# Retention and a mixture of experts in one kernel: slots and gates of quarter rows fetched through DRAM, drains spread over the experts, other capacities

## The chip, the cores and the metric

The kernel runs on one core of one Trainium2 chip. The metric is the device time of one execution in microseconds (us): the median of three timed runs before the change is 395.25 us (395.16 to 395.92). A further run was taken with the hardware profiler, and its own time is given beside its span. Engine names are those of the profile: PE is the matrix engine (PEld its weight loads), DVE the vector engine, ACT the scalar engine, POOL the general one, SP the engine that issues most DMAs; a name with a q (POOLq) is the engine's queue.

## The reference

```
# retention: 8 sequences, 8 heads, 576 positions, 64 wide
scores = q @ k^T / sqrt(64);  ret = scores * gamma_h ** (i - j) for i >= j, else 0
x = (ret @ v) as 4608 rows of 512
# mixture of experts with a skip
active = x @ w_skip > 0;  out = x
e = argmax(x[active] @ w_gate) over 8 experts;  gate = its softmax probability
out[active] = x[active] + gate * (relu(x[active] @ w1[e]) @ w2[e])   # 512 -> 1024 -> 512
```

## The kernel before

**Retention.** The first 158 us compute x, 36 tiles of 128 tokens by 512, and write it to out. On the way each token gets an expert and a rank in it. The experts are then handled in the order of their token counts (the busiest first), each with a fixed number of columns from `CAPS`; tokens beyond a capacity would go to a loop at the end, which runs zero times on the reference's inputs.

**Expert 0** is special: 256 of its rows are gathered and multiplied during the last retention tiles (`up_early`, `down_early`), the rest, `CAPS[0] - 256` rows, is the late block (`up_late`). Its weights come in pieces: ACT makes a high part, and POOL the low part of a half chunk in `lower`, which is called with one or two pieces per retention tile. The two copies of the gathered rows by chunk, xp (L430, POOL), feed the turns `pt_early` (L841) on PE.

**Experts 1 to 7** run through eight chunks f of the hidden layer. A step is an up (12 matmuls into ph) and, one step later, a down (12 matmuls into py): all products are three-term products of high and low parts, so each expert has 192 matmuls that stream its capacity in columns. After an up ACT writes the high part hhi and DVE the low part hlo (L570); the down reads hhi in its first matmul and hlo in its second. Weights of a chunk are loaded by SP (w), split by ACT (whi) and DVE (wlo, L187).

**Quarter rows.** A token's 512 features are handled as four quarters of 128. For an expert e from 2 on, `gather_next` fetches its token rows (xg, POOL indirect DMA), `stow` writes them to DRAM (xr, L1215), `spread` reads them back as quarters (xq, four DMAs on SP's queue, L1225), and `turn_quarters` (DVE, L1239) turns them into the columns of the up. The results of experts 1 to 6 are turned by DVE out of PSUM (yq), scaled by the gates on ACT (`scale_quarters`, L1136), added to xq on DVE (`add_quarters`, L1144), and written by POOL as indirect puts (L1147), 60 in all. `quarter_ids` makes the destination rows qidx and the gates qgate of all experts: 16 matmuls of idf and gate with a selector sel spread them over the partitions (ps_q, L1105), and DVE works on them. `slot_first` broadcasts the first slot's ids by two matmuls (ps_first, L511), for the slots without a token.

**Order.** The order on each engine is written by hand: `at(e, f, place, ...)` hangs an action on step (e, f), place 0 after the up of f, place 1 after the down of f - 1, place 2 after the weights' splits and loads. `keep` holds that order. A group (`new_group`, `in_line`) keeps POOL's indirect DMAs in sequence. A single drain of POOL (L1301) stands at (7, 3, 1).

**End.** After expert 7's last down, py is copied to SBUF (two groups by ACT, two by DVE), turned by 12 transposes into three blocks yn, and DVE makes rs = yn * gate + xg for each (L1188); POOL puts each to out (L1192). All this is `finish`. The loop at L1402 and the end of the kernel (L1498) follow.

Of the kernel before, what the change touches and what calls it, by code (L numbers as in the profile page):

```python
# [11 lines left out]
F32 = mybir.dt.float32  # L12
# [5 lines left out]
ALU = mybir.AluOpType  # L18
# [13 lines left out]
NQD = P // Q  # L32
NBLK = 3

CAPS = (368, 344, 332, 308, 304, 286, 278, 276)
CAP = CAPS[0]
MAXB = -(-NTOK // P)
NW = NE + 1
# [16 lines left out]
LOADED = (6, 8, 10, 11, 12, 13)  # L55
KCUT = 3
LAST = len(GROUPS) - 1
CUT = 2 * P
EARLY = ("sc0", "sc1", "s", "xt0", "xt1", "sc0")
NCUT = 6  # L60
# [5 lines left out]
def kernel(  # L66
# [402 lines left out]

    gidx = const.tile([P, NBLK, NE], I32, tag="gidx", name="gidx")  # L470
    sidx = const.tile([P, NBLK, NE], I32, tag="sidx", name="sidx")
    gate = const.tile([P, NBLK, NE], F32, tag="gate", name="gate")

    def late_ids(ps):

# [21 lines left out]
    def slot_ids(ps):  # L497

        info = ps[:, 0 : NBLK * NE * NCMP].rearrange("s (b e k) -> s b e k", b=NBLK, k=NCMP)
        vec("tensor_copy", raw, info)  # L500
        idf = rt.tile([P, NBLK, NE], F32, tag="idf", name="idf")
# [6 lines left out]
    def slot_first(idf):  # L508

        ps = bank("m", "ps_first")[:, :NE]  # L510
        nc.tensor.matmul(ps, row, idf[0:1, 0, :], start=True, stop=True)  # L511
        return ps

    def slot_rest(idf, first):

        some = rt.tile([P, NBLK, NE], F32, tag="some_slot", name="some_slot")
        head = first.unsqueeze(1).broadcast_to([P, NBLK, NE])
        vec("scalar_tensor_tensor", some, idf, float(P), head, ALU.is_lt, ALU.mult)
        vec("tensor_tensor", some, some, idf, ALU.add)
        vec("tensor_scalar", near, some, float(-P), 0.0, ALU.add, ALU.max)  # L520
        far = rt.tile([P, NBLK, NE], F32, tag="far", name="far")
        vec("tensor_scalar", far, idf, float(P), FAR, ALU.is_lt, ALU.mult)
        vec("scalar_tensor_tensor", sidx, idf, float(-P), far, ALU.add, ALU.add)
        gs = rt.tile([P, NBLK, NE], F32, tag="gs", name="gs")
        vec("tensor_tensor", gs, raw[:, :, :, 2], raw[:, :, :, 3], ALU.add)
        vec("tensor_tensor", gs, gs, raw[:, :, :, 4], ALU.add)
        by = in_order(gs, "gates")
        vec("tensor_reduce", gate, by, axis=AX.X, op=ALU.add)

    row = const.tile([1, P], F32, tag="row", name="row")  # L530
    nc.gpsimd.memset(row, 1.0)
# [65 lines left out]
    with ExitStack() as actx:  # L597
# [322 lines left out]
        for g in range(NT):  # L920
# [18 lines left out]
            if not last:  # L939
                first = decayed(g, pxt)  # L940
                scale(g + 2, first)
                lower(1 if g < NT - 6 else 2, first)
            score(g + (AHEAD_SC if g > 2 else 1))
            if g < 4:
                decays(g + 1)
# [44 lines left out]

    xg0.append(mp.tile([P, DM], F32, tag="xg0_2", name="xg0_2", bufs=1))
    nblock = None
    sel = None
# [3 lines left out]
    qgate = mp.tile([P, NQD * NQE], F32, tag="qgate", name="qgate", bufs=1)  # L997
# [77 lines left out]

    def quarter_tables():

        nonlocal sel
# [21 lines left out]
    def quarter_ids(idf):  # L1100

        ps = bank("m", "ps_q")[:, : 2 * NQD * NQE].rearrange("p (x j i) -> p x j i", x=2, j=NQD)
        for x, t in enumerate((idf, gate)):
            for j in range(NQD):
# [3 lines left out]
        yield  # L1108
        ids = ps[:, 0].rearrange("p j i -> p (j i)")
        t = mp.tile([P, NQD * NQE], F32, tag="t", name="t", bufs=1)  # L1110
        vec("tensor_scalar", t, ids, float(P), 4 * FAR, ALU.is_lt, ALU.mult)
        vec("tensor_tensor", t, t, none, ALU.add)
        vec("scalar_tensor_tensor", t, ids, float(NQD), t, ALU.mult, ALU.add)
        vec("tensor_scalar", qidx, t, quarter, None, ALU.add)
        vec("tensor_copy", qgate, ps[:, 1].rearrange("p j i -> p (j i)"))

    def results(e):
        return mp.tile([P, -(-CAPS[1] // Q), P], F32, tag="yq", name=f"yq_{e}", bufs=1)
# [12 lines left out]

    def scale_quarters(e, yq, gs):

        gates = qgate.rearrange("p (j k e) -> p j k e", j=NQD, e=NE)
# [26 lines left out]
        puts.append(put)  # L1161

    def evacuate(e, py):
        if e == 0:
            return py
        m = CAPS[e]
        yT = results(e).rearrange("p g f -> p (g f)")[:, : NCC * m].rearrange("p (c i) -> p c i", c=NCC)
        for c in range(NCC):
            if c % 2:
                keep(nc.vector.tensor_copy(yT[:, c, :m], py[c][:, :m]))  # L1170
            else:
                keep(nc.scalar.copy(yT[:, c, :m], py[c][:, :m]))
        return yT

    def rows(xg, k, n):
        return xg[k][:n] if isinstance(xg, list) else xg[:n, k, :]

    def finish(e, y, xg, ks, tags=("pt", "m")):
        new_group()
        for k, n in ks:  # L1180
            if e == 0:
                yn = y[k]
            else:
                yn = bank(tags[k % len(tags)], f"yn_{e}_{k}")
                for c in range(NCC):
                    nc.tensor.transpose(chunk(yn[:n], c), y[:, c, k * P : k * P + n], ident)
            rs = mp.tile([P, DM], F32, tag="rs", name=f"rs_{e}_{k}", bufs=3)
            keep(nc.vector.scalar_tensor_tensor(rs[:n], yn[:n], gate[:n, k, e : e + 1], rows(xg, k, n), ALU.mult, ALU.add))  # L1188
            put_rows(e, k, n, rs)

    def put_rows(e, k, n, rs):
# [27 lines left out]
    def spread(e):  # L1219

        n = span(e)
        xq[e] = mp.tile([P, NBLK * NCC, P], F32, tag="xq", name=f"xq_{e}", bufs=2)
        for q in range(NQD):
            rows = xr[e][:, q * P : (q + 1) * P].rearrange("(g a) f -> a g f", a=Q)
            keep(nc.sync.dma_start(xq[e][q * Q : (q + 1) * Q, : n // Q, :], rows))  # L1225

    def copy_rows(e, xg):

        xq[e] = mp.tile([P, NBLK * NCC, P], F32, tag="xq", name=f"xq_{e}", bufs=2)
# [20 lines left out]
    def experts():  # L1250
# [74 lines left out]
        first = []  # L1325
        at(0, NCUT - 2, 1, lambda: first.append(slot_first(idf)))
        at(0, NCUT - 1, 1, lambda: slot_rest(idf, first[0]))
        at(0, NCUT, 1, rank_caps)
        for cur in steps + [None]:
            if cur:  # L1330
# [16 lines left out]
            if last:  # L1347
# [4 lines left out]
                if f == NFC - 1:  # L1352
                    if 0 < e < NE - 1:
                        yq, n = turn_out(e, py[e]), span(e) // Q
                        head, rest = range(NQD), range(NQD, n)
                        at(e + 1, 0, 2, scale_quarters, e, yq, head)
                        at(e + 1, 1, 0, add_quarters, e, yq, xq[e], head)
                        at(e + 1, 1, 0, scale_quarters, e, yq, rest)
                        at(e + 1, 2, 0, add_quarters, e, yq, xq[e], rest)
                    else:  # L1360
                        finish(e, evacuate(e, py[e]), xg[e], blocks(e), ("pt", "m", "ph"))
            for do in between.pop((*place, 1), ()) if place else ():
                do()
            if cur:
# [139 lines left out]
```

## Time and profile before

| | |
|---|---|
| median of 3 runs | 395.25 us (395.16 to 395.92) |
| the profiled execution | 392.77 us, of which its span is 391.1 us |
| mean granted PE clock | 0.995 |
| busy of the span | PE 96%, DVE 68%, POOL 47%, ACT 41% |
| retention; expert 0 and the start of 1 | to about 158 us; to about 186 us |
| experts 1 to 7 | about 186 to 381 us |
| after the last matmul of py | 381 to 391 us |

The shares are means over stages. An engine's idle time counts only where another one waits for it, so the waits of PE and the stretch behind its last matmul are to be read first.

### The profile page before, as it was taken

What the parts mean: (1) busy time and instruction counts of PE and PEld (TensorE: products, weight loads), DVE (VectorE), ACT (ScalarE), POOL (GpSimd) and SP (SyncE); (2) the same over time, 40 slices, a digit from 0 to 9 for tenths busy, and PEclk for the clock granted to TensorE, in tenths of its full rate; (3) what the DMA queues carried; (4) which work ended last, traced back from release to release, by engine and by line L of the source; (5) the groups of instructions that cost most, each with busy time, mean ns of one, the idle gap of its engine ahead of it and who ended that gap; (6) DMA issues with size and microseconds to landing.
All of it is one profiled execution on the core that took longest, in us unless ns stands there. A gap on an engine that the chain in (4) does not pass through costs nothing.

```text
span 391.1 us, 12059 instructions
## 1 busy us (share of the span) xinstructions
PE 374.3 (96%) x4786; PEld 339.8 (87%) x4786; DVE 266.4 (68%) x606; ACT 159.0 (41%) x312; POOL 185.7 (47%) x253
## 2 busy tenths in 40 slices
PE   8989999999899999999999999999999999999991
PEld 4768788788688778888998999999999999999990
DVE  3765694695497945759654876876977788759622
ACT  1213222232223354126242673573564656636520
POOL 5433242342242587259650048547567188470633
PEclk9999999999999999999999999999999999999998
DMA  7999999999999665063999669759678976895001
GB/s 278 389 374 362 359 392 344 341 385 373 386 358 363 215 202 169 26 204 140 290 344 237 173 222 277 244 184 288 227 231 260 279 221 249 251 300 166 30 31 57
DMA packets 50795, 99.97 MB, mean 256 GB/s; under 512 B 6255, under 2 KB 15219, under 8 KB 50736
## 3 DMA queue, kind: packets, MB, share of 16 engines
q1 hardware_dynamic: 41232, 79.58, 62.2%
q0 software_dynamic: 4032, 10.03, 7.9%
q10 hardware_dynamic: 5472, 9.56, 6.5%
q8 instruction: 39, 0.64, 0.7%
q14 instruction: 20, 0.16, 0.1%
HBM read 80.44 MB, written 19.21 MB: 255 GB/s over the span
## 4 chain that ended last, share of the span: by engine, by line
PE 70%; DMA 12%; DVE 6%; POOL 5%; issue 4%; ACT 1%; SPq 1%; POOLq 0%; ACTq 0%; DVEq 0%
PE py L546 19%; PE ph L546 17%; PE pxt L751 8%; PE psc L679 6%; PE px L802 5%; PE ps_s L729 4%; PE pxt L772 4%; DMA out<-yq,qidx 4%; DMA xq<-xr 2%; PE pl L810 2%; DMA xg<-out,near 2%; PE ph_early L546 2%; DMA xg<-out,gidx 2%; DMA xr<-xg 1%; DVE sc L199 1%
## 5 line engine op out<-in xcount | busy, mean ns | idle before, releaser
L1147 POOL DMA_INDIRECT out<-yq,qidx x60 | 69.6, 1160 | 82.6 <-ACT yq L1136 66.8
L187 DVE TENSOR_TENSOR wlo_w<-w,whi_w 128x1024 fp32r<-128x1024 f32 x58 | 70.4, 1214 | 17.6 <-ACT whi_w L184 17.2
L714 POOL TENSOR_TENSOR v<-v,tt_sb 128x512 f32<-128x512 f32 x36 | 37.5, 1042 | 80.5 <-DVE xt L199 58.4
L546 PE MATMUL py<-hlo,whi_w 128*128 128x344 f32 (+6 forms) x224 | 68.1, 304 | 1.4 <-DVE hlo L570 1.4
L546 PE MATMUL ph<-xhi,whi_w 128*128 128x344 f32 (+6 forms) x224 | 67.8, 303 | 0.0
L546 PE MATMUL ph<-xhi,wlo_w 128*128 128x344 f32 (+6 forms) x224 | 67.8, 303 | 0.0
L546 PE MATMUL py<-hhi,whi_w 128*128 128x344 f32 (+6 forms) x224 | 67.8, 303 | 0.0
L546 PE MATMUL py<-hhi,wlo_w 128*128 128x344 f32 (+6 forms) x224 | 67.7, 302 | 0.0
L546 PE MATMUL ph<-xlo,whi_w 128*128 128x344 f32 (+6 forms) x224 | 67.7, 302 | 0.0
L184 ACT CAST whi_w<-w 128x1024 fp32r<-128x1024 f32 x58 | 60.4, 1045 | 4.7 <-DMA w<-w 4.7
L199 DVE TENSOR_TENSOR xt<-pxt,gt_sb 128x256 f32<-128x256 f32 x72 | 27.1, 417 | 36.3 <-PE pxt L772 33.8
L199 DVE TENSOR_TENSOR sc<-psc,mask 128x512 f32<-128x512 f32 x72 | 46.3, 684 | 7.4 <-POOL v L714 4.5
L569 ACT ACTIVATE hhi<-ph 128x344 fp32r<-128x344 f32 (+7 forms) x58 | 24.5, 422 | 60.5 <-PE ph L546 60.5
L804 ACT COPY xn<-px 128x512 f32<-128x512 f32 x36 | 21.1, 587 | 64.4 <-PE px L802 54.2
L546 PEld LDWEIGHTS py<-hlo,whi_w 128*128 128x128 f32 x224 | 42.2, 189 | 2.2 <-DVE hlo L570 2.2
L546 PEld LDWEIGHTS ph<-xhi,whi_w 128*128 128x128 f32 x224 | 42.2, 188 | 0.1
L546 PEld LDWEIGHTS ph<-xlo,whi_w 128*128 128x128 f32 x224 | 42.2, 188 | 0.1
L546 PEld LDWEIGHTS py<-hhi,whi_w 128*128 128x128 f32 x224 | 42.3, 189 | 0.0
L546 PEld LDWEIGHTS py<-hhi,wlo_w 128*128 128x128 f32 x224 | 42.2, 189 | 0.0
L546 PEld LDWEIGHTS ph<-xhi,wlo_w 128*128 128x128 f32 x224 | 42.2, 188 | 0.0
L751 PE MATMUL pxt<-sc,v 128*64 128x128 f32 x576 | 40.0, 275 | 0.3 <-DVE sc L199 0.2
L570 DVE SCALAR_TENSOR_TENSOR hlo<-ph,hhi 128x344 fp32r<-128x344 f32 (+7 forms) x58 | 27.2, 468 | 18.4 <-ACT hhi L569 18.4
(226 smaller groups left out, 621.1 us busy)
## 6 DMA issues: line engine op xcount, KB each, us to landing
w<-w SPq DMA_DIRECT2D x64, 512.0 KB, 4.8
q<-qkv SPq DMA_DIRECT2D x72, 256.0 KB, 5.5
v<-qkv SPq DMA_DIRECT2D x68, 256.0 KB, 5.4
out<-xn ACTq DMA_DIRECT2D x36, 256.0 KB, 5.4
xr<-xg SPq DMA_DIRECT2D x7, 512.0 KB, 4.8
xq<-xr SPq DMA_DIRECT2D x12, 144.0 KB, 5.1
xq<-xr SPq DMA_DIRECT2D x8, 176.0 KB, 6.8
xq<-xr SPq DMA_DIRECT2D x8, 160.0 KB, 5.8
```

The source lines that it names most:

```text
L184: cast = nc.scalar.copy(hi, t)
L187: ins = nc.vector.tensor_tensor(lo, t, hi.bitcast(F32), ALU.subtract)
L199: ins = getattr(nc.vector, name)(*args, **kw)
L546: nc.tensor.matmul(ps, x, y, start=first and n == 0, stop=last and n == 3 * len(terms) - 1)
L569: keep(nc.scalar.activation(hi, ph, AF.Relu))
L570: keep(nc.vector.scalar_tensor_tensor(lo, ph, 0.0, hi.bitcast(F32), ALU.max, ALU.subtract))
L679: nc.tensor.matmul(psc[r][halves[c], a, k0:], q[halves[r], 1, a, k0 : k0 + D], q[halves[r], 0, a, k0:], start=a == 0, stop=a == NPR - 1, s ...
L714: ins = nc.gpsimd.tensor_tensor(v, v, vt_sb[:, place(g), :].unsqueeze(2).broadcast_to([P, H, D]), ALU.mult)
L751: nc.tensor.matmul(pxt[a % 2][halves[j], a // 2, :], v[:, head(a, r), :], sc[:, r, a, :], start=a < 2, stop=t == 0 and a >= NPR - 2, skip_ ...
L802: nc.tensor.transpose(px[:, c * P : (c + 1) * P], xt_t[b][:, c, o * P : (o + 1) * P], ident)
L804: nc.scalar.copy(xn, px)
L1147: nc.gpsimd.indirect_dma_start(out=rows, out_offset=bass.IndirectOffsetOnAxis(ap=ids[:, g % NQD, g // NQD, e : e + 1], axis=0), in_=yq[:, ...
```

## The change

It does five things. (1) `slot_first` and the matmuls ps_q go. The slots' ids and gates lie in one tile, `slots`, which SP writes to DRAM after stow(1) at (0, 7, 1) and reads back in four DMAs at (1, 1, 0), so that each partition has the ids and gates of its four quarters; `quarter_ids` works on these at (1, 3, 0). The id of a slot without a token is taken from the partition's own first slot. (2) Drains of POOL stand at (e, 5, 1) for e = 2 to 6 beside the one at (7, 3, 1). (3) Expert 7 ends in `finish_last`: three column groups are turned and added first and the fourth after them, ACT copies the fourth group in two pieces, and DVE copies one group only. (4) `CAPS` changes. (5) The last retention tiles call `lower` no more before the copies of xp, so those pieces go behind them. Besides, `add_quarters` for the rest of the quarters moves from (e + 1, 2, 0) to (e + 1, 1, 2).

```diff
-CAPS = (368, 344, 332, 308, 304, 286, 278, 276)
+CAPS = (380, 344, 320, 310, 300, 288, 278, 268)
...
-    gate = const.tile([P, NBLK, NE], F32, tag="gate", name="gate")
+    slots = const.tile([P, 2, NBLK, NE], F32, tag="slots", name="slots")
+    gate = slots[:, 1]
...
-        head = first.unsqueeze(1).broadcast_to([P, NBLK, NE])
+        head = idf[:, 0:1, :].broadcast_to([P, NBLK, NE])
...
-                lower(1 if g < NT - 6 else 2, first)
+                if g < NT - 3:
+                    lower(1 if g < NT - 6 else 2, first)
...
-        sel = mp.tile([P, DM], F32, tag="rs", name="sel", bufs=3).rearrange("p (j i) -> p j i", j=NQD)
-        for j in range(NQD):
-            part = ident[:, j * Q : (j + 1) * Q].unsqueeze(1).broadcast_to([P, NQD, Q])
-            pool("tensor_copy", sel[:, j].rearrange("p (q a) -> p q a", a=Q), part)
...
-                nc.tensor.matmul(
-                    ps[:, x, j, :], sel[:, j, :], t.rearrange("p k e -> p (k e)"), start=not (x or j), stop=True, skip_group_check=True
-                )
...
+    def store_slots():
+        kept = dp.tile([P, 2 * NQE], F32, tag="slots", name="kept", bufs=1)
+        keep(nc.sync.dma_start(kept, slots.rearrange("p x k e -> p (x k e)")))
+        return kept
+    def quarter_slots(kept):
+        rows = kept.rearrange("(j a) i -> a j i", a=Q)
+        for q in range(NQD):
+            keep(nc.sync.dma_start(qslot[q * Q : (q + 1) * Q], rows))
...
+    def finish_last(e, y, xg, ks):
+        yn = [bank(tag, f"yn_{e}_{tag}") for tag in ("pt", "m", "ph")]
+        rs = [mp.tile([P, DM], F32, tag="rs", name=f"rs_{e}_{k}", bufs=3) for k, n in ks]
+        cuts = (0, NCC - 1), (NCC - 1, NCC)
+        for c0, c1 in cuts:
+            for k, n in ks:
+                for c in range(c0, c1):
+                    nc.tensor.transpose(chunk(yn[k][:n], c), y[:, c, k * P : k * P + n], ident)
+        new_group()
+        for k, n in ks:
+            for c0, c1 in cuts:
+                out, a, b = (
+                    t.rearrange("p (q c b) -> p q c b", q=NQD, c=NCC)[:, :, c0:c1] for t in (rs[k][:n], yn[k][:n], xg[:n, k, :])
+                )
+                keep(nc.vector.scalar_tensor_tensor(out, a, gate[:n, k, e : e + 1], b, ALU.mult, ALU.add))
+            put_rows(e, k, n, rs[k])
...
-        at(NE - 1, 3, 1, new_group)
-        at(NE - 1, 3, 1, lambda: tc.keep_in_program_order(nc.gpsimd.drain()))
+        for e in range(2, NE):
+            at(e, 3 if e == NE - 1 else 5, 1, new_group)
+            at(e, 3 if e == NE - 1 else 5, 1, lambda: tc.keep_in_program_order(nc.gpsimd.drain()))
...
-        ids = quarter_ids(idf)
-        at(1, 0, 0, next, ids)
-        at(1, 1, 0, next, ids, None)
+        kept = []
+        at(0, NFC - 1, 1, lambda: kept.append(store_slots()))
+        at(1, 1, 0, lambda: quarter_slots(kept[0]))
+        at(1, 3, 0, quarter_ids)
...
-                        at(e + 1, 2, 0, add_quarters, e, yq, xq[e], rest)
+                        at(e + 1, 1, 2, add_quarters, e, yq, xq[e], rest)
```

## Rows read from the trace of the kernel before

**Rows 1.** Page, part 4: the chain of waits by engine, shares of the span.
```profile
PE 70%; DMA 12%; DVE 6%; POOL 5%; issue 4%; ACT 1%; SPq 1%; POOLq 0%; ACTq 0%; DVEq 0%
```
**Rows 2.** Stretch of experts 1 to 7: length, busy by engine, clock, DMA share, GB/s.
```profile
218.00:380.80 162.80, 162.14 (x1178) 161.57 (x1177) 120.50 (x229) 88.46 (x178) 88.57 (x88) 1.00 0.69 215
```
**Rows 3.** Chain in time (start, us, what): blocks at 344 and 278 columns.
```profile
222.31 1.90 PE py L546 x12
...
351.24 1.55 PE ph L546 x12
```
**Rows 4.** Timeline of POOL (start, us, operation): low parts and copies of xp.
```profile
142.05 1.40 POOL L862 TENSOR_TENSOR wlo_w<-w,whi_w 128x256 fp32r<-128x256 f32 x2
143.40 1.16 POOL L430 COPY xp<-xg 128x512 f32<-128x512 f32 x2
```
**Rows 5.** Timeline of PE at the same place (brackets: idle before, and releaser).
```profile
144.06 0.33 PE L841 MATMUL pt_early<-ident,xp 128*128 128x128 f32 x1 [0.51 <-POOL xp L430]
144.61 0.33 PE L841 MATMUL pt_early<-ident,xp 128*128 128x128 f32 x1 [0.23 <-POOL xp L430]
```
**Rows 6.** Timeline of PE: ps_first.
```profile
176.51 0.38 PE L511 MATMUL ps_first<-idf,row 1*128 1x8 f32 x2
```
**Rows 7.** Stretch of ps_q, line 1105 alone: length, PE and PEld busy, clock, DMA.
```profile
188.47:190.17 1.70, 1.70 (x16) 1.70 (x16) 1.00 1.04 399
```
**Rows 8.** Chain in time: POOL's copies for the selector.
```profile
175.92 0.97 POOL sel L205 x4
```
**Rows 9.** Page, part 5: casts of weights (busy, mean ns, idle before, releaser).
```profile
L184 ACT CAST whi_w<-w 128x1024 fp32r<-128x1024 f32 x58 | 60.4, 1045 | 4.7 <-DMA w<-w 4.7
```
**Rows 10.** Timeline of DVE: the first turn of expert 2.
```profile
213.19 0.55 DVE L1239 STREAM_TRANSPOSE xt<-xq 128x352 f32<-128x352 f32 x1 [1.81 <-DMA xq<-xr]
```
**Rows 11.** Timeline of PE: the down that follows.
```profile
214.19 0.42 PE L546 MATMUL py<-hlo,whi_w 128*128 128x344 f32 x1 [0.73 <-DVE hlo L570]
```
**Rows 12.** Waits of PE (us in total, times, longest).
```profile
PE py L546 <- DVE hlo L570: 1.4, 3, 0.7
```
**Rows 13.** Stretch before that turn, columns as in rows 2.
```profile
186.00:216.00 30.00, 29.27 (x185) 28.39 (x184) 16.47 (x26) 9.87 (x16) 11.42 (x12) 1.00 1.07 295
```
**Rows 14.** Page, part 3: SP's DMA queue (packets, MB, share of 16 engines).
```profile
q1 hardware_dynamic: 41232, 79.58, 62.2%
```
**Rows 15.** Timeline of DVE: hlo and rest add in experts 2 and 7.
```profile
231.83 0.50 DVE L570 SCALAR_TENSOR_TENSOR hlo<-ph,hhi 128x332 fp32r<-128x332 f32 x1
232.24 1.08 DVE L1144 TENSOR_TENSOR yq<-yq,xq 128x896 f32<-128x896 f32 x1
...
365.05 0.44 DVE L570 SCALAR_TENSOR_TENSOR hlo<-ph,hhi 128x276 fp32r<-128x276 f32 x1
365.41 0.81 DVE L1144 TENSOR_TENSOR yq<-yq,xq 128x640 f32<-128x640 f32 x1
366.14 1.22 DVE L187 TENSOR_TENSOR wlo_w<-w,whi_w 128x1024 fp32r<-128x1024 f32 x1
```
**Rows 16.** Timeline of PE: the matmuls that read these hlo first.
```profile
233.34 0.31 PE L546 MATMUL py<-hlo,whi_w 128*128 128x332 f32 x1
...
365.69 0.29 PE L546 MATMUL py<-hlo,whi_w 128*128 128x276 f32 x1
```
**Rows 17.** Line 1301: duration ns min/median/max, first and last start.
```profile
L1301 POOLq DRAIN  x1: 13579/13579/13579, 369.9 to 369.9; - x1
```
**Rows 18.** Timeline of POOL behind the drain.
```profile
383.50 0.10 POOL L205 MEMSET step_on<- 128x1 f32 x1 [7.28 <-issue]
384.33 0.98 POOL L1192 DMA_INDIRECT out<-rs,sidx  x1 [0.73 <-DVEq L1402]
```
**Rows 19.** Line 1498, columns as in rows 17: drains at the kernel's end.
```profile
L1498 POOLq DRAIN  x3: 46/103/297, 389.9 to 390.8; - x3
```
**Rows 20.** Timeline of POOL: the shortest idle between a gather and the next puts.
```profile
338.10 1.01 POOL L1147 DMA_INDIRECT out<-yq,qidx  x1 [4.62 <-ACT yq L1136]
```
**Rows 21.** Timeline of DVE: the three rs of expert 7.
```profile
381.93 2.06 DVE L1188 SCALAR_TENSOR_TENSOR rs<-yn,gate,xg 128x512 f32<-128x512 f32 x3 [0.42 <-PE yn L1186]
```

More of the change, by code (lines that the diff above doesn't have):

```diff
@@ L57 @@
 LAST = len(GROUPS) - 1
+XQ = 2
 CUT = 2 * P
@@ L500, in slot_ids @@
         vec("tensor_copy", raw, info)
-        idf = rt.tile([P, NBLK, NE], F32, tag="idf", name="idf")
+        idf = slots[:, 0]
         vec("scalar_tensor_tensor", idf, raw[:, :, :, 0], float(P), raw[:, :, :, 1], ALU.mult, ALU.add)
@@ L506, in slot_ids, with slot_rest @@
         return idf
[L508 to L514, printed above, removed]
+    def slot_rest(idf):
         some = rt.tile([P, NBLK, NE], F32, tag="some_slot", name="some_slot")
-        head = first.unsqueeze(1).broadcast_to([P, NBLK, NE])
+        head = idf[:, 0:1, :].broadcast_to([P, NBLK, NE])
         vec("scalar_tensor_tensor", some, idf, float(P), head, ALU.is_lt, ALU.mult)
@@ L528, in slot_rest @@
         vec("tensor_reduce", gate, by, axis=AX.X, op=ALU.add)
-    row = const.tile([1, P], F32, tag="row", name="row")
-    nc.gpsimd.memset(row, 1.0)
     near = const.tile([P, NBLK, NE], I32, tag="near", name="near")
@@ L992 @@
     nblock = None
-    sel = None
     NQE = NBLK * NE
@@ L996 @@
     qidx = mp.tile([P, NQD * NQE], I32, tag="qidx", name="qidx", bufs=1)
-    qgate = mp.tile([P, NQD * NQE], F32, tag="qgate", name="qgate", bufs=1)
+    qslot = mp.tile([P, NQD, 2 * NQE], F32, tag="qslot", name="qslot", bufs=1)
     quarter = mp.tile([P, 1], F32, tag="quarter", name="quarter", bufs=1)
@@ L1076, in quarter_tables @@
     def quarter_tables():
-        nonlocal sel
-        sel = mp.tile([P, DM], F32, tag="rs", name="sel", bufs=3).rearrange("p (j i) -> p j i", j=NQD)
-        for j in range(NQD):
-            part = ident[:, j * Q : (j + 1) * Q].unsqueeze(1).broadcast_to([P, NQD, Q])
-            pool("tensor_copy", sel[:, j].rearrange("p (q a) -> p q a", a=Q), part)
         p = pidx[:, 0:1]
@@ L1098, in quarter_tables, with quarter_ids @@
             pool("tensor_scalar", beyond[:, :, :, e], slot, float(CAPS[e]), 4 * FAR, ALU.is_ge, ALU.mult)
[L1100 to L1104, printed above, removed]
-                nc.tensor.matmul(
-                    ps[:, x, j, :], sel[:, j, :], t.rearrange("p k e -> p (k e)"), start=not (x or j), stop=True, skip_group_check=True
-                )
-        yield
-        ids = ps[:, 0].rearrange("p j i -> p (j i)")
-        t = mp.tile([P, NQD * NQE], F32, tag="t", name="t", bufs=1)
+    def store_slots():
[6 more added lines that the diff above has]
+            keep(nc.sync.dma_start(qslot[q * Q : (q + 1) * Q], rows))
+    def quarter_ids():
+        ids = qslot[:, :, :NQE]
+        t = mp.tile([P, NQD, NQE], F32, tag="t", name="t", bufs=1)
         vec("tensor_scalar", t, ids, float(P), 4 * FAR, ALU.is_lt, ALU.mult)
-        vec("tensor_tensor", t, t, none, ALU.add)
+        vec("tensor_tensor", t, t, none.rearrange("p (j i) -> p j i", j=NQD), ALU.add)
         vec("scalar_tensor_tensor", t, ids, float(NQD), t, ALU.mult, ALU.add)
-        vec("tensor_scalar", qidx, t, quarter, None, ALU.add)
-        vec("tensor_copy", qgate, ps[:, 1].rearrange("p j i -> p (j i)"))
+        vec("tensor_scalar", qidx.rearrange("p (j i) -> p j i", j=NQD), t, quarter, None, ALU.add)
     def results(e):
@@ L1132, in scale_quarters @@
     def scale_quarters(e, yq, gs):
-        gates = qgate.rearrange("p (j k e) -> p j k e", j=NQD, e=NE)
+        gates = qslot[:, :, NQE:].rearrange("p j (k e) -> p j k e", e=NE)
         for g in gs:
@@ L1163, in evacuate @@
     def evacuate(e, py):
-        if e == 0:
-            return py
         m = CAPS[e]
@@ L1168, in evacuate, with finish @@
         for c in range(NCC):
-            if c % 2:
+            if c == 1:
                 keep(nc.vector.tensor_copy(yT[:, c, :m], py[c][:, :m]))
             else:
-                keep(nc.scalar.copy(yT[:, c, :m], py[c][:, :m]))
-        return yT
-    def rows(xg, k, n):
-        return xg[k][:n] if isinstance(xg, list) else xg[:n, k, :]
-    def finish(e, y, xg, ks, tags=("pt", "m")):
+                for c0, c1 in ((0, P), (P, m)) if c == NCC - 1 else ((0, m),):
+                    keep(nc.scalar.copy(yT[:, c, c0:c1], py[c][:, c0:c1]))
+        return yT
+    def finish_last(e, y, xg, ks):
[6 more added lines that the diff above has]
+                    nc.tensor.transpose(chunk(yn[k][:n], c), y[:, c, k * P : k * P + n], ident)
         new_group()
         for k, n in ks:
[L1181 to L1186, printed above, removed]
+            for c0, c1 in cuts:
[4 more added lines that the diff above has]
+            put_rows(e, k, n, rs[k])
+    def finish(e, yn, xg, ks):
+        new_group()
+        for k, n in ks:
             rs = mp.tile([P, DM], F32, tag="rs", name=f"rs_{e}_{k}", bufs=3)
-            keep(nc.vector.scalar_tensor_tensor(rs[:n], yn[:n], gate[:n, k, e : e + 1], rows(xg, k, n), ALU.mult, ALU.add))
+            keep(nc.vector.scalar_tensor_tensor(rs[:n], yn[k][:n], gate[:n, k, e : e + 1], xg[k][:n], ALU.mult, ALU.add))
             put_rows(e, k, n, rs)
@@ L1221, in spread @@
         n = span(e)
-        xq[e] = mp.tile([P, NBLK * NCC, P], F32, tag="xq", name=f"xq_{e}", bufs=2)
+        xq[e] = mp.tile([P, NBLK * NCC, P], F32, tag="xq", name=f"xq_{e}", bufs=XQ)
         for q in range(NQD):
@@ L1227, in copy_rows @@
     def copy_rows(e, xg):
-        xq[e] = mp.tile([P, NBLK * NCC, P], F32, tag="xq", name=f"xq_{e}", bufs=2)
+        xq[e] = mp.tile([P, NBLK * NCC, P], F32, tag="xq", name=f"xq_{e}", bufs=XQ)
         for k, n in blocks(e):
@@ L1319, in experts @@
         at(1, 0, 0, spread, 1)
-        ids = quarter_ids(idf)
-        at(1, 0, 0, next, ids)
-        at(1, 1, 0, next, ids, None)
+        kept = []
+        at(0, NFC - 1, 1, lambda: kept.append(store_slots()))
+        at(1, 1, 0, lambda: quarter_slots(kept[0]))
+        at(1, 3, 0, quarter_ids)
         at(0, 0, 0, down_early, NCUT - 1)
         at(0, 1, 1, split_raw, 1)
-        first = []
-        at(0, NCUT - 2, 1, lambda: first.append(slot_first(idf)))
-        at(0, NCUT - 1, 1, lambda: slot_rest(idf, first[0]))
+        at(0, NCUT - 1, 1, slot_rest, idf)
         at(0, NCUT, 1, rank_caps)
@@ L1358, in experts @@
                         at(e + 1, 1, 0, scale_quarters, e, yq, rest)
-                        at(e + 1, 2, 0, add_quarters, e, yq, xq[e], rest)
+                        at(e + 1, 1, 2, add_quarters, e, yq, xq[e], rest)
+                    elif e:
+                        finish_last(e, evacuate(e, py[e]), xg[e], blocks(e))
                     else:
-                        finish(e, evacuate(e, py[e]), xg[e], blocks(e), ("pt", "m", "ph"))
+                        finish(e, py[e], xg[e], blocks(e))
             for do in between.pop((*place, 1), ()) if place else ():
```

## The prediction

> **What bounds the kernel now.** I read the chain of waits first, then the stretches of time, then the timelines of the places that the diff touches. The chain is mostly TensorE [rows 1]. In the expert stage PE is busy 162.14 of 162.80 us [rows 2]: what counts there is a matmul taken away, or a wait put in front of one. Blocks of 12 matmuls follow each other with no gap, and their length goes with the columns: 1.90 us at 344, 1.55 at 278 [rows 3], so 0.35 / 66 = 0.0053 us per column and block, and 16 blocks per expert make 0.085 us per column of a capacity. After the last matmul the end is POOL's: a drain, then three puts one behind the other (rows below). So every edit is priced either on PE's path or in this tail. All prices come from the profiled execution (392.77 us, a span of 391.1 and 1.7 around it); the median of the timed runs is 2.5 above it, and I subtract the sum from the median.
>
> **The change, part by part.**
>
> *Low parts behind the copies of xp.* Two POOL low parts run from 142.05 to 143.45, ahead of the two copies of xp [rows 4], and PE waits 0.51 and 0.23 for these copies, with only a few matmuls between the waits [rows 5]. Behind the copies, the low parts no longer delay them: at most 1.4. The gathered rows that the copies read must have landed as well, which these rows don't show, so I take -1.1, between the waits (-0.7) and the low parts (-1.4). The low parts moved are read by the up products of expert 0 several us later; that lead, by the code, is their cover. If it were gone, the 1.4 would come back.
>
> *Capacities.* Experts 1 to 7 lose 12 + 4 + 8 and gain 2 + 2 columns: 20 net, 20 x 0.085 = -1.7. The late block of expert 0 grows from 112 to 124 rows: 24 matmuls with 24 columns more, 24 with 12 more, and two whole ups with 12 more; at 0.0053 / 12 us per column and matmul that is 0.25 + 0.13 + 0.13 = +0.5. Expert 2's span falls from 352 to 320 rows, so one put goes.
>
> *ps_first.* Two short matmuls, 0.38 together, of which PE loses 0.3: -0.3 [rows 6]. The DVE operations behind it stay.
>
> *Quarters' slots and gates.* The 16 matmuls ps_q fill PE from 188.47 to 190.17 [rows 7]: -1.7. POOL also loses the four copies that built their selector, 0.97 [rows 8], and so it gathers expert 2's rows sooner. DVE loses one small copy. SP gains five issues, some 0.5 each, ahead of spread(2) and of weights. The weights are loaded well ahead: of 58 casts two waited for one, 4.7 in all [rows 9]; that lead covers the issues, and without it their 2 us would stand before PE. The new cost is in the DMA. Expert 2's turned rows (xq) are already late: DVE idles 1.81 for them, the low part hlo stands behind that turn on DVE [rows 10], and PE waits 0.73 for hlo [rows 11]. The three waits of PE on hlo sum to 1.4 [rows 12]; one follows at the next turn, one is at xq of expert 7. The stretch before it has the DMA engines at a share of 1.07 [rows 13]: this xq lands when the transfers ahead of it have passed, not when PE asks. PE arrives there 1.1 + 0.3 + 1.7 - 0.5 = 2.6 earlier. The xq comes earlier by its sooner gather (the 1.1 and about 1 for the selector) and by its smaller capacity, 2.2 in all, less what the new small transfers take. These are 128 pieces of 192 bytes into DRAM and 4 x 128 back. By bytes (123 KB at the 295 GB/s of that stretch [rows 13]) they take 0.4; at the mean packet time of the main queue (62.2% of 16 x 391.1 us over 41,232 packets: 94 ns [rows 14]) 640 / 16 x 94 ns = 3.8, though its packets are some ten times as large. No row shows a packet of this size, so I take 1.0, nearer the end by bytes, and keep both. The wait then grows by 2.6 - 2.2 + 1.0 = +1.4 (0.8 to 4.2).
>
> The Trainium skill (DMA: Bandwidth & Descriptors, Specifications) says that below 512 bytes a DMA does a read-modify-write and misses line rate. That speaks for the dear end; no row of this kernel separates it, and by it alone this term would be the +4.2.
>
> *Rest of the quarters added one step sooner.* Before, DVE ran low part of the weights, hlo, rest add. Now the add stands ahead of hlo. There is no gap to hold it: hlo follows its predecessor at once in expert 7 (no idle is noted), ends at 365.49, and the add hands over 0.73 after its start [rows 15]. PE needs this hlo in the second matmul of its down, at 365.69 [rows 16]: 0.20 of slack, so a wait of 0.53. In expert 2 hlo ends at 232.33, the add takes 1.08 in full and somewhat less to the next start, and PE reads at 233.34: 0 [rows 15, 16]. The six experts by the same sum: 0, 0.56, 0.30, 0.71, 0.55, 0.53, together +2.65 (0 to +3.2; 0 if ACT's work shifts so that a gap opens). These waits stand in front of PE one expert at a time, and nothing gives them back but xq of expert 7, which then comes in time: -0.5, about a third of [rows 12]. The puts start only about 0.4 sooner, off the path.
>
> *Drains.* One drain at 369.9 lasts 13.58 us in the queue [rows 17]. Its part behind POOL's last put is the idle 7.28 that ends at 383.50, followed by 0.73 before the first put [rows 18]. At the end three more indirect DMAs are drained, and the longest of three drains takes 0.297 against 0.046 for the shortest [rows 19]: 0.084 per DMA. Before the first drain 87 indirect DMAs were issued: 87 x 0.084 = 7.3, the idle. So I read it as a cost per DMA since the last drain. The six drains then have 29, 13, 13, 13, 9 and 9 DMAs behind them: 2.4, 1.1, 1.1, 1.1, 0.8, 0.8. The first five fall in POOL's idle between a gather and the next expert's puts, whose shortest is 4.62 [rows 20]; queued behind them are only these puts. The last ends long before PE does.
>
> *Last turns by column group.* Without the drain, the first put waits for its rs only. Before, the three rs run from 381.93 for 2.06 [rows 21], so the first is ready at 382.68 and a put could start near 382.8, 1.5 before 384.33 [rows 18]. The two cuts let the first part of rs start before the fourth column group is copied, perhaps 0.2 sooner; they also make PE turn that group last, and if a reader of part of the bank waits for all of it, 0.3 is lost. The puts keep their spacing. I take -1.5 (-1.2 to -1.8).
>
> **The sum.** -1.1 - 1.7 + 0.5 - 0.3 - 1.7 + 1.4 + 2.65 - 0.5 - 1.5 = -2.25. Forecast: 395.25 - 2.25 = 393.0.
>
> **The rivals.**
>
> *A, the drain has a fixed price.* If one drain costs 7.3 whatever stands before it, the last one again ends after PE: issued at about 375 it is done near 382.5, and the tail gains about 0.6 in place of 1.5. The drains in the shorter gaps delay puts by up to 2.7, and the next expert's results need the buffer that these empty, which I put at +0.8. Sum -0.6: 394.7. For it: only one long drain was ever seen. Against it: the short drains, which fit the count. The Trainium skill (GPSIMD Engine Reference, 2.1 Instruction dispatch) gives the first call of newly loaded code about 6 us with no instruction shown; by it the drain's price would be paid once, earlier, and the sum would stand as forecast.
>
> *B, the rest add is hidden.* If DVE finds a gap, the +2.65 goes: -4.9, 390.35. Against it: no idle in the rows at hlo. For it: PE's blocks shift against ACT's scaling in every expert.
>
> *C, slower: the small transfers hold back xq of expert 2.* Place: the first turn of expert 2, in the stretch where the engines are full. At 94 ns per piece the wait grows by 4.2 in place of 1.4: -2.25 + 2.8 = +0.55, and with the rest adds at their upper bound (+3.2) +1.1: 396.3. It decides from some 80 ns per piece on, where the gains are used up. For it: the saturation; against it: the pieces are a tenth of the mean packet.
>
> *D, the change loses its cover in the tail:* the last drain or the evacuation by ACT alone of the fourth group delays rs, and the tail gains nothing: -0.75, 394.5, within the noise.
>
> **How the numbers follow.** Forecast 0.50 (its own range 391.8 to 394.3), B 0.17, A 0.10, D 0.08, C 0.15. A difference of 0.2%, 0.8 us, is about what a measurement of this kernel tells from none. A and D count mostly as no change, C as slower in 0.11 and no change in 0.04; a twentieth of the forecast's share falls under 0.8. Faster 0.70, same 0.18, slower 0.12. The range reaches from somewhat below B, 390.0, to just short of C, 395.9.
>
> **What would show it.** Right: no ps_first and ps_q on PE; the copies of xp start near 142.1; PE's waits on hlo grow from 1.4 to about 5 in all, some six of them at the third step of an expert, with the rest add ahead of hlo on DVE; six drains of 2.4, about 1 and under 1 us; the first last put within 0.2 of the first rs. Wrong: drains of 7 us each (A), no wait at the third step (B), xq of expert 2 landing at its old time or later (C), a first put long after its rs (D). A PE that waits somewhere else for weights, after SP's five issues, would break the sum in a way that I have priced at nothing.

## The result, and the profile after

The changed kernel is slower: 1.0105 of the time before (95% interval 1.0068 to 1.0142), 4.2 us at a median of 396.5 for the kernel before in the same comparison. 393.0 was forecast, and a range that ended at 395.9. The profiled execution has a span of 398.3 us and a mean granted clock of 0.991. Ratios compare fast runs, those within 1.5% of the fastest of their kernel; three of the profiles below (112 late rows, last put of 16 rows, one drain) are of slower runs, and of these only single waits and stretches are read.

The two spans differ by 7.2 us, more than the medians do. The table cuts them by the starts of PE's first matmuls of each stretch (by the puts at the end), after less before:

| stretch | before | after | |
|---|---|---|---|
| retention, up to the px ahead of the early turns | 142.89 | 145.53 | +2.64 |
| to the first early turn (pt_early) | 1.17 | 0.49 | -0.68 |
| to the first late up of expert 0 | 23.53 | 26.63 | +3.10 |
| to the first up of expert 1 | 19.01 | 18.73 | -0.28 |
| to the first up of expert 2 | 33.72 | 35.80 | +2.08 |
| experts 2 to 7 | 160.54 | 160.66 | +0.12 |
| first turn of the last rows to the first put | 3.47 | 2.55 | -0.92 |
| last put to the end | 4.17 | 5.33 | +1.16 |

The first row is not the change's: in the 14 profiles of this study that stretch took 141.6 to 148.3, with nearly the same code in it, and the profile of before is among the short ones. The rest sums to +4.6, near the +4.2 of the timed runs. That nearness is in part luck: each kernel has one profile, and other rows vary too (experts 2 to 7 took 160.7 to 162.7 in the six profiles with the rest add and the capacities of the changed kernel there). Two stretches hold most of the loss, and in neither had the forecast put a price of that size; the end adds 1.2.

Page of after, part 4, the chain by engine, against [rows 1]: PE's share fell from 70% to 52%, and DMA's rose from 12% to 22%. By the same page 9 of these 22 points are q<-qkv, a load of the retention, which the change doesn't touch.
```profile
PE 52%; DMA 22%; DVE 9%; issue 5%; ACT 5%; POOL 3%; SPq 2%; POOLq 1%; ACTq 0%; DVEq 0%
```
Waits of PE in after (us in total, times, longest), against [rows 12]. The second line was not there before.
```profile
PE py L540 <- DVE hlo L564: 4.3, 5, 2.5
PE pt L1055 <- ACT xp L431: 2.7, 1, 2.7
...
PE py L540 <- ACT hhi L563: 0.9, 1, 0.9
```
**The late rows of expert 0.** Timeline of POOL in before and in after: the gather of the late rows takes 2.47 us to issue in place of 1.08.
```profile
160.65 1.08 POOL L435 DMA_INDIRECT xg<-out,gl  x1 [3.30 <-DVE gl L199]
```
```profile
162.74 2.47 POOL L436 DMA_INDIRECT xg<-out,gl  x1 [3.32 <-DVE gl L200]
```
DMA issues of before and of after (last number: us from issue to landing):
```profile
xg<-out,gl POOLq DMA_INDIRECT x1, 3.4
```
```profile
xg<-out,gl POOLq DMA_INDIRECT x1, 7.2
```
Timeline of PE there: the turn of these rows waits 2.67 for their copy, which follows the landing.
```profile
170.64 0.54 PE L1055 MATMUL pt<-ident,xp 124*128 124x124 f32 x3 [2.67 <-ACT xp L431]
```
**Expert 1.** Timeline of DVE in after, against [rows 10]: it stands 7.49 us in front of quarter_ids, for the slots read back from DRAM. The weights' low part and hlo are queued behind. The wait for xq of expert 2 that follows is only 0.92. The four reads take SP 3.46 us to issue (timeline of SP) and land a median of 9.4 us behind their issue.
```profile
213.49 0.21 DVE L200 TENSOR_SCALAR t<-qslot 128x96 f32<-128x96 f32 x1 [7.49 <-DMA qslot<-kept]
...
218.28 0.51 DVE L1240 STREAM_TRANSPOSE xt<-xq 128x320 f32<-128x320 f32 x1 [0.92 <-DMA xq<-xr]
```
```profile
202.21 3.46 SPq L1099 DMA_DIRECT2D qslot<-kept  x4
```
```profile
qslot<-kept SPq DMA_DIRECT2D x4, 24.0 KB, 9.4
```
Timeline of PE there, against [rows 11]:
```profile
213.34 0.43 PE L540 MATMUL py<-hhi,whi_w 128*128 128x344 f32 x1 [0.86 <-ACT hhi L563]
216.28 0.42 PE L540 MATMUL py<-hlo,whi_w 128*128 128x344 f32 x1 [2.51 <-DVE hlo L564]
```
Two stretches of it (length, busy by engine, clock, DMA share, GB/s): PE is busy 0.90 of 4 us, and in the next four the granted clock is 0.58, a mean of its two levels, 2.4 and 1.2 GHz. The wait costs a second time there. At the wait for the late rows the clock of this profile stays at 1.00.
```profile
212.00:216.00 4.00, 0.90 (x5) 0.38 (x3) 2.34 (x6) 2.69 (x4) 0.00 (x0) 1.00 0.85 205
216.00:220.00 4.00, 3.73 (x14) 3.73 (x15) 2.95 (x6) 0.46 (x1) 0.00 (x0) 0.58 1.01 367
```
**The other parts.** Early turns (timeline of PE, against [rows 5]): no wait for xp is left.
```profile
146.03 1.04 PE L835 MATMUL pt_early<-ident,xp 128*128 128x128 f32 x8
```
Rest add (timeline of DVE in expert 7, against [rows 15]): add first, then hlo, which PE gets 0.67 late.
```profile
371.81 0.82 DVE L1137 TENSOR_TENSOR yq<-yq,xq 128x640 f32<-128x640 f32 x1
372.55 0.43 DVE L564 SCALAR_TENSOR_TENSOR hlo<-ph,hhi 128x268 fp32r<-128x268 f32 x1
```
```profile
373.03 0.39 PE L540 MATMUL py<-hlo,whi_w 128*128 128x268 f32 x1 [0.67 <-DVE hlo L564]
```
The tail (timeline of POOL, against [rows 18]): behind the last drain POOL is idle 1.51 in place of 7.28 and then waits for rs, not for the drain. The first rs starts at 389.24 (timeline of DVE), just behind the turn of the fourth column group of its block (388.93 to 389.20), though its own three groups were turned by 388.4.
```profile
384.48 0.10 POOL L206 MEMSET step_on<- 128x1 f32 x1 [1.51 <-issue]
390.40 0.98 POOL L1193 DMA_INDIRECT out<-rs,sidx  x1 [5.82 <-DVE rs L1182]
```
Behind the five drains in the experts POOL is idle 4.98, 4.19, 3.12, 5.04 and 3.12; two of them:
```profile
263.43 0.10 POOL L206 MEMSET step_on<- 128x1 f32 x1 [4.98 <-issue]
...
344.56 0.10 POOL L206 MEMSET step_on<- 128x1 f32 x1 [5.04 <-issue]
```
The first rs:
```profile
389.24 0.88 DVE L1182 SCALAR_TENSOR_TENSOR rs<-yn_pt,slots,xg 128x384 f32<-128x384 f32 x2 [1.50 <-PE yn_pt L1175]
```

### The profile page after: what moved, and what is told of

Read it like the earlier page. It is cut to its first block, busy times and chain, and to the rows that moved or that the text cites. A ratio compares the mean times of both kernels' runs of the same rounds, so it can differ in the third digit from the quotient of the medians.

```text
span 398.3 us, 12026 instructions
## 1 busy us (share of the span) xinstructions
PE 372.9 (94%) x4768; PEld 337.7 (85%) x4768; DVE 266.2 (67%) x599; ACT 159.0 (40%) x313; POOL 183.8 (46%) x252
## 4 chain that ended last, share of the span: by engine, by line
PE 52%; DMA 22%; DVE 9%; issue 5%; ACT 5%; POOL 3%; SPq 2%; POOLq 1%; ACTq 0%; DVEq 0%
PE py L540 15%; PE ph L540 14%; DMA q<-qkv 9%; PE pxt L745 5%; DMA out<-yq,qidx 4%; PE psc L673 3%; PE ps_s L723 3%; PE pxt L766 3%; PE px L796 3%; ACT yq L1129 3%; DVE yq L1120 2%; DMA qslot<-kept 2%; DMA xg<-out,near 2%; DMA xg<-out,gl 2%; PE pl L804 1%
## 5 line engine op out<-in xcount | busy, mean ns | idle before, releaser
L564 DVE SCALAR_TENSOR_TENSOR hlo<-ph,hhi 128x344 fp32r<-128x344 f32 (+7 forms) x58 | 27.3, 471 | 25.0 <-ACT hhi L563 24.7
```

Source lines behind the costliest of these rows:

```text
L564: keep(nc.vector.scalar_tensor_tensor(lo, ph, 0.0, hi.bitcast(F32), ALU.max, ALU.subtract))
```

## The experiments

Theory 1, formed on the trace: DVE's wait for the slots is the loss. Rivals: the xq of expert 2 is late whoever waits; the rest adds are the loss; the late block of 124 rows is. All ratios are to the kernel before, and each kernel has one profile.

**Ids later.**
```diff
-        at(1, 3, 0, quarter_ids)
+        at(1, 7, 0, quarter_ids)
```


> quarter_ids moved from (1, 3, 0) to (1, 7, 0), all else as changed. Theory 1 (DVE stands in quarter_ids waiting for qslot, idle 7.5 us, and the low parts behind it hold PE up for 5.4 us): the idle before quarter_ids on DVE goes, PE waits on hlo of expert 1 no longer than the wait for xq of expert 2 lasts, some 2 to 3 us, and the time is about 2.5 us below that of the changed kernel, ratio to before near 1.004. Rival 2 (the small transfers hold back xq of expert 2, whoever waits for them): xq of expert 2 still lands about 5 us after PE needs it, no gain. Rival 3 (the rest adds ahead of hlo are the loss): nothing changes, ratio 1.010.


1.0112 (1.0073 to 1.0151): no gain. DVE's wait for the slots is gone, but xq of expert 2 is turned 26.9 us after expert 1's first up, as in after, and DVE waits for it:
```profile
219.70 0.51 DVE L1240 STREAM_TRANSPOSE xt<-xq 128x320 f32<-128x320 f32 x1 [1.75 <-DMA xq<-xr]
```
PE's waits in expert 1 fall only from 3.4 us (2.5 for hlo, 0.9 for hhi) to 2.6, and the stretch from 35.8 to 35.0. Theory 1 falls as the whole cause: behind the wait for the slots stood one for xq.

**Slots behind spread(2).**
```diff
-        at(1, 1, 0, lambda: quarter_slots(kept[0]))
-        at(1, 3, 0, quarter_ids)
+        at(1, 3, 0, lambda: quarter_slots(kept[0]))
+        at(2, 0, 0, quarter_ids)
```


> quarter_slots behind spread(2), at (1, 3, 0), and quarter_ids at (2, 0, 0). Theory 1: no wait for qslot on DVE at all and xq of expert 2 comes some 2 us sooner than with the ids alone moved, since SP issues its four reads before the small ones; PE waits in expert 1 for about 1 us or less; 4.5 us below the changed kernel, ratio to before about 0.998. Rival 2: the same gain, but with the ids alone moved there was none. Rival 3: ratio stays 1.010.


1.0190 (1.0137 to 1.0243), a miss: not faster. The stretch from expert 1 to 2 is 34.3 in place of 35.8, but the first turn of xq comes at 27.3, and the turn of the late rows still waits 2.6. By time it is 3.4 us slower than the changed kernel, which its profile doesn't explain.

**Rest add back.**
```diff
-                        at(e + 1, 1, 2, add_quarters, e, yq, xq[e], rest)
+                        at(e + 1, 2, 0, add_quarters, e, yq, xq[e], rest)
```


> The rest add of the quarters back at (e + 1, 2, 0), behind hlo, all else as changed. Rival 3: PE's waits at the third step of experts 2, 4, 5 and 7 (0.5, 0.6, 0.9, 0.95) go, 2.9 us below the changed kernel, ratio about 1.003, while the wait for qslot stays. If theory 1 were all of the loss: no change, ratio 1.010. Both causes can hold side by side.


1.0052 (1.0008 to 1.0096). Expert by expert, 2 to 7, the stretches are shorter than in after by 0.44, 0, 0.57, 0.89, 0 and 0.73: 2.6 us. The timed gain is 2.1, but the intervals of the two ratios overlap, so only the stretches show it. Of PE's five waits on hlo two are left, both in expert 1.
```profile
PE py L540 <- DVE hlo L564: 3.4, 2, 3.0
```

**Both.** The two edits above together.


> Slots behind spread(2), ids at (2, 0, 0) and the rest add back at (e + 1, 2, 0). If both causes hold and add up: 7 us below the changed kernel, 3 us below the kernel before, ratio about 0.992. If the rest add matters little: as with the slots alone, about 0.998. If neither is the cause: 1.010.


1.0072 (1.0038 to 1.0107): not additive, and not below 1. In this profile the turn of the late rows waits 2.8, xq of expert 2 is turned 28.1 after the first up, and the stretch is 36.25. Something else was still in all four kernels.

**Late block of 112 rows.**
```diff
-CAPS = (380, 344, 320, 310, 300, 288, 278, 268)
+CAPS = (368, 344, 320, 310, 300, 288, 278, 268)
```


> The changed kernel with the first capacity back at 368, so that the late block has 112 rows in place of 124; the rest as changed. Theory 4 (a gather of 124 rows, no multiple of 16, is the loss before expert 1: its issue takes 2.5 us in place of 1.1, it lands 7.2 us after it in place of 3.4, and PE waits 2.7 for the late turn): the issue takes 1.1 again, the wait of the late turn goes, the stretch from the early turns to the late up is 23.5 us in place of 26.6 to 29.3; at least 3 us below the changed kernel, ratio about 1.002. Rival 5 (the low parts moved behind the copies hold POOL or PE up there): the stretch stays near 27, and the time falls by the 0.4 of the columns only.


1.0050 (1.0009 to 1.0091), 2.2 us below the changed kernel where 3 were expected, and the intervals overlap. The wait of the late turn is gone, the issue of the gather is 1.08 and the stretch to the late up 24.6.

**Last put of 16 rows.**
```diff
-CAPS = (380, 344, 320, 310, 300, 288, 278, 268)
+CAPS = (380, 344, 320, 310, 300, 288, 278, 272)
```


> The changed kernel with the last capacity 272 in place of 268: the last put has 16 rows in place of 12. In all five profiles with 268 the end came 5.0 to 5.6 us after the start of the last put, against 4.2 with 20 rows before. Theory 6 (the number of rows of that put makes its landing longer): back to about 4.2, less 0.3 for four more columns, 0.8 us below the changed kernel, ratio about 1.008. Rival 7 (it is the code after it, or chance): 5.3 stays, ratio 1.011.


1.0137 (1.0079 to 1.0195); the end comes 5.2 after the last put, so the number of its rows is not what made it longer.

**One drain.**
```diff
-        for e in range(2, NE):
-            at(e, 3 if e == NE - 1 else 5, 1, new_group)
-            at(e, 3 if e == NE - 1 else 5, 1, lambda: tc.keep_in_program_order(nc.gpsimd.drain()))
+        at(NE - 1, 3, 1, new_group)
+        at(NE - 1, 3, 1, lambda: tc.keep_in_program_order(nc.gpsimd.drain()))
```


> The changed kernel with the single drain at (7, 3, 1), the five others taken out. Theory 8 (a drain costs about 0.08 us for each indirect DMA since the last one): POOL is idle for some 7 us behind its last put before the three last ones, the first of which starts 3.4 us after the first turn in place of 2.55, or 1 us later; ratio about 1.013. Rival 9 (the drains between delay the puts and the gathers, and cost time): faster than the changed kernel, by up to 2 us.


1.0209 (1.0144 to 1.0273). Timeline of POOL: the idle of 7.20 is back, for 86 DMAs 0.084 each. It delays the first put by 0.6 (3.15 after the first turn in place of 2.55); the rest of its time is hidden by PE's last down and the turns. By time this kernel is 4.1 us slower than the changed one, and the intervals just miss each other: the trace accounts for 0.6 of it, and the rest is open.
```profile
397.54 0.10 POOL L206 MEMSET step_on<- 128x1 f32 x1 [7.20 <-issue]
398.37 0.98 POOL L1193 DMA_INDIRECT out<-rs,sidx  x1 [0.73 <-DVE rs L1182]
```

**Five parts on the kernel before.** No slots through DRAM, no earlier rest add, 112 late rows.
```diff
-CAPS = (368, 344, 332, 308, 304, 286, 278, 276)
+CAPS = (368, 344, 320, 310, 300, 288, 278, 272)
...
-        head = first.unsqueeze(1).broadcast_to([P, NBLK, NE])
+        head = idf[:, 0:1, :].broadcast_to([P, NBLK, NE])
...
-                lower(1 if g < NT - 6 else 2, first)
+                if g < NT - 3:
+                    lower(1 if g < NT - 6 else 2, first)
...
+                    elif e:
+                        finish_last(e, evacuate(e, py[e]), xg[e], blocks(e))
```
The six drains are those of the changed kernel.


> The kernel before with five parts of the change: low parts behind the copies of xp, no ps_first, six drains, the last turns by column group, and the capacities 368, 344, 320, 310, 300, 288, 278, 272; without the slots through DRAM, the larger late block and the earlier rest add. If theories 1 (or its rival 2), 3 and 4 name all that was lost: 0.7 + 0.3 + 0.9 + 1.4 below the kernel before, some 3 us, ratio about 0.992. If one of the parts kept is a loss: 1.0 or more.


0.9953 (0.9906 to 0.9999): faster than the changed kernel, and than the kernel before by 1.9 us, just clear of none, where some 3 were expected. Some of the missing 1.1 can be seen: the early turns start 0.68 sooner, but the stretch from them to the late up is 24.16 in place of 23.53. PE comes sooner to a matmul that needs a mask of the routing (mks) from DVE and waits longer there (waits of PE before, then here):
```profile
PE ps_m L281 <- DVE mks L199: 0.4, 1, 0.4
```
```profile
PE ps_m L281 <- DVE mks L199: 1.1, 1, 1.1
```

**Late block of 108 rows.**
```diff
-CAPS = (380, 344, 320, 310, 300, 288, 278, 268)
+CAPS = (364, 344, 320, 310, 300, 288, 278, 268)
```


> The changed kernel with the first capacity at 364: a late block of 108 rows, fewer than the 112 of before, but no multiple of 16. Theory 4a (it is the multiple of 16): the gather of the late rows issues for about 2.5 us and lands some 7 us after its start as with 124 rows, PE waits about 2.7 us for the late turn. Rival 4b (it is the larger number of rows): 1.1 us, no wait, as with 112.


1.0100 (1.0057 to 1.0143). Between the two theories: the issue takes 2.17, and the rows land after 4.5, but PE doesn't wait; the lead covers 1.1 us more, not 3.8. Fewer rows than 112 are slower to gather than 112, and less slow than 124. By time there is no gain over 124 rows, though the wait is gone; the intervals leave room for 2 us either way.
```profile
162.92 2.17 POOL L436 DMA_INDIRECT xg<-out,gl  x1 [3.33 <-DVE gl L200]
```

*What the three row counts do.* The semaphore of the gather is raised 16 times as it lands. With 112 rows all 16 come 2.9 to 3.4 us after the issue began (five profiles). With 108 four come at 3.2 to 3.3 and twelve at 4.0 to 4.5. With 124 twelve come at 3.6 to 3.8 and four at 6.1 to 7.3, in all eight profiles. The packet records fit this: the rows go in pairs of 4,096 bytes, and the single rows of 2,048 left over are 16, 12 and 4. In after the packets follow each other in four chains, a pair each 155 ns. So I read 16 lanes (parts of the transfer that run side by side) of 7 rows, 12 of 9 and 4 of 31, and 124 is slow because four lanes carry it all. 16, 12 and 4 are the largest numbers up to 16 that divide 112, 108 and 124; no other size was tried.

**Slots through DRAM on the five parts.** Read back at (1, 3, 0), used at (2, 0, 0).
```diff
-        ids = quarter_ids(idf)
-        at(1, 0, 0, next, ids)
-        at(1, 1, 0, next, ids, None)
+        kept = []
+        at(0, NFC - 1, 1, lambda: kept.append(store_slots()))
+        at(1, 3, 0, lambda: quarter_slots(kept[0]))
+        at(2, 0, 0, quarter_ids)
```


> The five parts kept in the kernel before (the run with the capacities 368 to 272), and with them the slots and gates through DRAM, read back behind spread(2) and used at (2, 0, 0), so that DVE waits for nothing there: part 1 alone. From the first up of expert 1 to that of expert 2 the run without it took 33.3 us, of which 1.7 are the 16 matmuls. Theory 10 (xq of expert 2 comes when the DMA has delivered it, whatever PE does, and the small transfers make it later): 33.3 or up to 1 more, the first turn still 26.5 to 28 us after the first up; PE's waits grow by the 1.7 that it saved; no faster than without the part. Rival 11 (what was lost there was the DVE's wait alone): 31.6 to 32.


0.9952 (0.9912 to 0.9991): by time no gain and no loss against the five parts alone, as theory 10 has it. Its one profile has the shortest stretch of all, 31.1 us, with the first turn of xq at 23.8 and no idle of DVE before it, as rival 11 has it. The two don't agree, and neither theory is shown.
```profile
187.03:218.17 31.14, 30.73 (x190) 30.02 (x189) 19.68 (x28) 13.57 (x21) 9.08 (x10) 1.00 0.97 299
```

**The same without the transfers.**
```diff
-        at(0, NFC - 1, 1, lambda: kept.append(store_slots()))
...
-        at(1, 3, 0, lambda: quarter_slots(kept[0]))
...
+        pool("memset", qslot, 0.0)
```


> The same without the store and the four reads of the slots: the slots are zero, so the results of the quarters of experts 1 to 6 are not written. Only the stretch from the first up of expert 1 to that of expert 2 is read. Theory 10, with the small transfers as the part that makes xq late: its first turn comes 1 us or more sooner than with them, and the stretch shrinks as much. If the transfers cost nothing there: the same turn, the same stretch, and the limit is the DMA's other work.


33.4 us and the first turn at 26.4: later without the transfers than with them. So these two profiles don't show the transfers holding xq back, and they differ by more than 2 us for a reason that is not known. The 31.1 above may be chance.
```profile
213.77 0.51 DVE L1241 STREAM_TRANSPOSE xt<-xq 128x320 f32<-128x320 f32 x1 [0.98 <-DMA xq<-xr]
```

**Late block of 124 rows alone.** On the five parts.
```diff
-CAPS = (368, 344, 320, 310, 300, 288, 278, 272)
+CAPS = (380, 344, 320, 310, 300, 288, 278, 272)
```


> The five parts kept in the kernel before (0.9953 of its time), with the first capacity at 380 again: the late block of 124 rows alone. Theory 4 (the indirect transfers of 124 rows are slow to make and to land): the gather of the late rows issues for 2.5 us, not 1.1, PE waits some 2.7 us for the late turn, and the whole is 3 us or more slower than with 112 rows, ratio to before 1.003 to 1.01. Rival 12 (the 124 rows only hurt beside the transfers of the slots, or their wait hides elsewhere): 0.995 to 0.997, the 0.5 of the columns.


1.0075 (1.0029 to 1.0121) against 0.9953: this one number costs 4.8 us, give or take 2.6 by the two intervals. Timeline of POOL in the five parts, then here; then the wait of PE, and the stretches around it, whose clock is 0.71 and 0.86:
```profile
162.49 1.08 POOL L435 DMA_INDIRECT xg<-out,gl  x1 [3.30 <-DVE gl L199]
```
```profile
162.17 2.47 POOL L435 DMA_INDIRECT xg<-out,gl  x1 [3.32 <-DVE gl L199]
```
```profile
PE pt L1054 <- ACT xp L430: 2.7, 1, 2.7
```
```profile
168.00:172.00 4.00, 1.85 (x7) 1.66 (x8) 0.13 (x1) 1.19 (x2) 3.00 (x4) 0.71 0.55 151
172.00:176.00 4.00, 4.00 (x22) 3.41 (x21) 2.16 (x7) 0.26 (x1) 3.12 (x11) 0.86 0.27 79
```
To the late up it takes 28.3 us in place of 24.2: 2.7 of wait, and the rest fits PE at the lower clock right behind it.

## Why the prediction was wrong

The forecast was -2.25 us, and +4.2 was measured. The step that failed is the late block in the capacities. "The late block of expert 0 grows from 112 to 124 rows" was priced by its matmuls' columns, at +0.5. Its rows come by an indirect DMA, and that step was put at nothing without a reason: 1.4 us more to issue, and 3.8 in all until it has landed, as four lanes carry what 16 carried; 2.7 of it reach PE. The eight profiles with 124 rows all have that wait, of 2.6 to 2.8; the six others none. In five of the eight a lower clock comes with it. Taken alone on the five parts it is 4.8 us by the timed runs (2.2 to 7.4). On the changed kernel 112 rows gained 2.2 by time and 108 rows 0.2, both give or take some 2.3. So the wait and its cause are shown, but not that they are the whole loss of 4.2.

The other steps:
- *Slots through DRAM*, forecast at -0.3 (-1.7 for ps_q, +1.4 for a longer wait for xq), measured +2.1 in that stretch. The place was right and the waiting instruction wrong: I had DVE wait for xq, and it waited 7.5 us for the slots, at quarter_ids, a wait that the change adds and that I did not name. SP's issues were wrong too: put at 0.5 each, the four reads took 3.46 us, and the last read of spread(2) went out 21.3 us behind the first up of expert 1 in place of 17.2. That is not what sets xq: with the slots behind, it went out at 18.7, and the first turn came at 27.3. Rival C's price per piece is refuted: the trace's packet records give 18 ns for one of 192 bytes, 0.7 us in all (640 / 16 x 18 ns). The rule that the Trainium skill states (DMA: Bandwidth & Descriptors, Specifications), that pieces under 512 bytes miss line rate, is not shown false by this, and the records agree with it: by the medians of after a piece of 192 bytes takes 15 ns (13 bytes per ns) and one of 2 KB 84 (24 bytes per ns); 640 of them are only too few to matter. Of the eleven profiles without ps_q, nine have a longer stretch than before (34.3 to 36.9 against 33.7), the one without transfers 33.4 and one 31.1: where xq ends last, the 1.7 that PE saves turn into a wait.
- *Rest add*: +2.65 forecast, 2.6 measured, though by experts 0.44, 0, 0.57, 0.89, 0, 0.73 in place of 0, 0.56, 0.30, 0.71, 0.55, 0.53: the sum is better than its terms, which is luck. Rival B fails.
- *Low parts*: -1.1 forecast; -0.68 to the turn, and the turns themselves take 0.5 less. But PE then waits 0.7 to 1.5 for mks in place of 0.4, in all thirteen other profiles, and without the late wait the stretch behind the turns is 0.6 to 1.5 longer than before (five profiles). So most of this gain, or all, is given back, which I had not looked for. *Columns* and *ps_first* about as forecast: with the rest add back, experts 2 to 7 take 158.0 in place of 160.5, of which 1.7 are columns and 0.7 the wait for xq of expert 7.
- *Drains*: rival A fails, since the last drain leaves POOL idle 1.51 and not 7. The price per DMA holds at 86 and 87 of them (0.084 each), but the six sizes were wrong: 4.98, 4.19, 3.12, 5.04, 3.12 and 1.51 in place of 2.4, 1.1, 1.1, 1.1, 0.8 and 0.8. The drain ends 0.7 to 1.1 us behind the last packet on POOL's queue where it follows 9 DMAs, 0.9 to 1.4 at 13, 1.6 to 2.3 at 29, and 6.4 and 6.5 at 86 and 87. So the count gives what comes behind the landing, and the forecast left the landing out.
- *Tail*: -1.5 forecast, -0.92 measured up to the first put. By the trace the drain was worth only 0.6 of it, and rs waits for the fourth group, the bound that I had at -1.2. After the last put +1.16 comes back. In all eleven profiles with the slots' code the end is 5.0 to 5.6 behind the last put, in the three without 4.0 to 4.2, and it stays so without the transfers (5.5). PE's branch at the loop takes 3.3 to 3.8 us in those eleven and 0.4 or less in the three: where the code lies is what I suspect, and it was not tried.

What stays open: why 108 rows gain nothing by time; whether the slots through DRAM gain anything with 112 rows; why one drain is 4.1 us slower by time; and the rest of what the five parts lacked.

## What to carry to other kernels

When a size changes, price every instruction that carries it, the transfers as well as the matmuls: the cheap-looking one may be on the path. Look at how the rows of a gather are shared out: here 112 rows landed sooner than 108. When a part that adds a transfer also adds its reader, ask what is queued behind that reader, and find the next wait behind it before counting on its removal. One part of a change can cost more than the others gain, so the parts are worth timing apart.

## What the runs showed of the hardware

An indirect gather of 112 rows of 2 KB issued in 1.08 us and landed after 3.3 to 3.4 with no packet of 8 bytes in the records; 108 rows took 2.17 and 4.5, with 16 such packets; 124 rows 2.47 and 7.1 to 7.3, with 180. The landing signals and the single rows give 16, 12 and 4 lanes at work, and the packets of 8 bytes fit the idle ones (4 x 4 and 12 x 15). A drain of POOL waited for the packets in flight and then took 0.05 to 0.12 us for each indirect DMA since the last drain (9 to 87 of them). A wait of PE of about 2.7 us came with a few us at 1.2 GHz in place of 2.4 in five of eight profiles, and in one pair of profiles the stretch grew by 1.4 us more than the wait.
